# Second attention's score transposes from TensorE to VectorE, paired scores, and a first batch in half chunks

## Chip, core and metric

The kernel runs on one core of one Trainium2 chip. The metric is the device time in microseconds of one execution.

## What is computed

Four batches of 8 heads, 576 queries, 64 dimensions, 32 pack vectors. First attention lets the packs attend to keys and values, second attention lets the queries attend to the packed result; the outcome is 2304 rows of 512. Two feed-forward layers of width 2048 follow, one with softplus, one with h times sigmoid(h). All inputs are fp32, and the weights come as 64-bit words that the kernel turns into fp32.

```
p_packed = sm_attn(p, k, v)
out = sm_attn(q, p_packed, p_packed)
x = out.transpose(0, 2, 1, 3).reshape(B * S, H * D)
g = softplus(x @ w_in);  x = g @ w_out
g = h * sigmoid(h) with h = x @ w_in2;  out = g @ w_out2
```

## The kernel before

Everything is kept transposed, with features on partitions and tokens along the free dimension. Layer 0 works on 8 blocks of 288 tokens (two a batch), layer 1 on blocks of 480. Each layer makes four passes f over the ff width, each with four chunks j of 128 (`GJ`). A unit is (layer, pass, block); a *step* is one chunk of one unit, and `run_steps` (L514) walks them. Step s emits six or twelve h matmuls (`emit_in`, L338) of its own chunk, then the y matmuls of one output quarter dm of the *previous* unit (`emit_out`, L378: four chunks with three matmuls each, 12). ScalarE applies the activation and makes the high part gh (`act_scalar`, L361), VectorE the low part gl (`act_vector`, L373), and `finish_out` (L393) copies or adds y into ya. So y of a unit needs gh and gl of all its chunks, and y starts in step 4. The tiles h and y have two PSUM buffers each.

In layer 0 the second attention's output is never formed: the matrix ax holds the normalised attention weights (32 packs x 4 head pairs on the 128 partitions, two head parities r), in a high and a low part, and `packed` (L317) multiplies each batch's pack vectors pt into the weights w_in, which gives vw. h is then vw times ax: (lo, hi), (hi, lo), (hi, hi), two matmuls each.

`att1(b)` (L168) computes scores of a parity with 8 matmuls of 64 x 32 x 288, takes the row maximum on VectorE, the exponential on ScalarE, transposes on TensorE (`turn`, L198), copies back (`turned`, L204; tile et has one buffer), weighs the values (`weigh`, L210) and turns the normalised result into pt. `att2(blk)` (L265) computes scores with the queries on 96 partitions (24 matmuls of 64 x 96 x 32), subtracts the maximum over the packs, exponentiates, sums, normalises (L284 to L295), and turns the result back with six TensorE transposes (L303); ScalarE copies the high part to ax (L308) and VectorE subtracts for the low part (L310). The scores' and transposes' PSUM tiles all come from one pool of two double banks (`two_banks`).

The work beside the steps is written as generators that yield the name of a point; `plan` (L91) puts them on an agenda by step, and within a step the points run as A0, h, PE, y, activation, A1, D0, D1, A2, D, then gl, then y's copy or addition. Weights are loaded by DMA some five steps before `conv_w` (L109) converts them: three integer passes on VectorE, and for all but the first layer's w_in a high and a low half. `plan_all` (L436) holds the table of steps. Ahead of step 0 stand att1(0), att2(0), att2(1), the first `packed` and eight weight conversions; the first four steps are put in order by an automatic scheduler (`NAUTO`), the rest stand as written. Att1(b) for b of 2 and 3 is planned for steps 8b-10 to 8b-5, att2 of its two blocks for 8b-4 to 8b.

Of the kernel before, what the change touches and what calls it, by code (L numbers as in the profile page):

```python
# [28 lines left out]
QT = 96  # L29
NQ = 3  # L30

N0 = NQ * QT
# [13 lines left out]
def body(ctx, tc, kT, vv, qT, pT, wi1, wo1, wi2, wo2, out):  # L46
# [25 lines left out]
    units = [(L, f, blk) for L in range(2) for f in range(NPASS) for blk in range(len(BLOCKS[L]))]  # L72
    US = {u: i for i, u in enumerate(units)}
    NS = GJ * len(units)
    at = lambda L, f, blk, i=0: GJ * US[L, f, blk] + i
    PER = [GJ * len(b) for b in BLOCKS]
    base = lambda L, f: at(L, f, 0)
# [82 lines left out]
    def load_q(blk):  # L160
        qt = att.tile([P, NQ, NK, QT], F32, name="qt", bufs=2)
        nc.sync.dma_start(out=qt, in_=qT[blk])
        qts[blk] = qt
# [4 lines left out]
    def att1(b):  # L168
# [5 lines left out]
        def scores(r):  # L174
            pz, kt = kts[b]
            s1[r] = two_banks()
            rows = slice(64 * r, 64 * r + 64)
            for half in range(2):
                for k in range(NK):
                    nc.tensor.matmul(  # L180
                        s1[r][32 * k:32 * k + 32, half, :HS], lhsT=pz[rows, k, :],
                        rhs=kt[rows, k, half * HS:(half + 1) * HS], start=True, stop=True,
                    )
# [20 lines left out]
        def turned(r):  # L204
            et[r] = att.tile([P, KC, P], F32, name="et")
# [16 lines left out]
        scores(0)  # L222
        yield "D"
        top(0)
        yield "A0"
        exp(0)
        yield "PE"
        scores(1)
        yield "D"
        top(1)  # L230
        yield "A0"
        exp(1)
        yield "PE"
        turn(0)
        yield "A1"
        turned(0)
        yield "D"
        nc.vector.tensor_copy(et[0][:64, 4, :], s1[0][:64, 1, :P])
        yield "PE"
        turn(1)  # L240
# [3 lines left out]
        yield "A1"  # L244
        turned(1)
        yield "D"
        nc.vector.tensor_copy(et[1][:64, 4, :], s1[1][:64, 1, :P])
        yield "PE"
# [16 lines left out]
    def att2(blk):  # L265

        b = blk // 2
        G = NQ * NK
        yield "PE"
        qt, pt = qts[blk], pts[b]  # L270
        tq = two_banks()
        for i in range(NQ):
            for k in range(NK):
                for r in range(NR):
                    rows = slice(64 * r, 64 * r + 64)
                    c = (i * NK + k) * NP
                    nc.tensor.matmul(  # L277
                        tq[:QT, r, c:c + NP], lhsT=qt[rows, i, k, :], rhs=pt[rows, k * NP:(k + 1) * NP],
                        start=True, stop=True,
                    )  # L280
        yield "D"
        tqv = tq[:QT, :, :G * NP].rearrange("q r (g p) -> q r g p", p=NP)
        mx = att.tile([QT, 2, NR, G], F32, name="mx", bufs=2)
        nc.vector.tensor_reduce(out=mx[:, 0], in_=tqv, axis=AX.X, op=ALU.max)  # L284
        ee = att.tile([QT, NR, G, NP], F32, name="ee", bufs=2)
        nc.vector.tensor_tensor(  # L286
            out=ee, in0=tqv, in1=mx[:, 0].unsqueeze(3).to_broadcast([QT, NR, G, NP]), op=ALU.subtract
        )
        yield "A0"
        nc.scalar.activation(out=ee, in_=ee, func=AF.Exp, scale=SCALE)  # L290
        yield "D"
        nc.vector.tensor_reduce(out=mx[:, 1], in_=ee, axis=AX.X, op=ALU.add)
        nc.vector.tensor_scalar(out=mx[:, 1], in0=mx[:, 1], scalar1=1e-9, scalar2=None, op0=ALU.add)
        nc.vector.reciprocal(out=mx[:, 1], in_=mx[:, 1])
        nc.vector.tensor_tensor(  # L295
            out=ee, in0=ee, in1=mx[:, 1].unsqueeze(3).to_broadcast([QT, NR, G, NP]), op=ALU.mult
        )
        yield "PE"
        tb = two_banks()
        ef = ee.rearrange("q r g p -> q r (g p)")  # L300
        for i in range(NQ):
            for r in range(NR):
                nc.tensor.transpose(  # L303
                    tb[:, r, i * QT:(i + 1) * QT], ef[:, r, i * P:(i + 1) * P], ident[:QT, :QT]
                )
        yield "A1"
        cols = slice(blk * N0, (blk + 1) * N0)
        nc.scalar.activation(out=ax[:, :NR, cols], in_=tb[:, :, :N0], func=AF.Copy)  # L308
        yield "D"
        nc.vector.tensor_tensor(  # L310
            out=ax[:, NR:, cols], in0=tb[:, :, :N0], in1=ax[:, :NR, cols].bitcast(F32), op=ALU.subtract
# [26 lines left out]
    def emit_in(s):  # L338
        L, f, blk = units[s // GJ]
        j = GJ * f + s % GJ  # L340
# [20 lines left out]
    def act_scalar(s, h):  # L361
        L, f, blk = units[s // GJ]
# [11 lines left out]
    def act_vector(s, gt, gh, gl):  # L374
        nc.vector.tensor_tensor(out=gl, in0=gt, in1=gh.bitcast(F32), op=ALU.subtract)  # L375
        gs[s] = gh, gl

    def emit_out(s):  # L378
        u, dm = s // GJ - 1, s % GJ
        L, f, blk = units[u]  # L380
        n = BLOCKS[L][blk][1]
        y = ps.tile([P, 512], F32, name="y")[:, :n]
        c = slice(dm * P, (dm + 1) * P)
        for jj in range(GJ):
            gh, gl = gs[GJ * u + jj]
            wh, wl = whl["o", L * NF + GJ * f + jj]
            for i, (w, g) in enumerate(((wl, gh), (wh, gl), (wh, gh))):
                nc.tensor.matmul(  # L388
                    y, lhsT=w[:, c], rhs=g, start=(jj == 0 and i == 0), stop=(jj == GJ - 1 and i == 2)
                )  # L390
        return y

    def finish_out(s, y):  # L393
        u, dm = s // GJ - 1, s % GJ
        L, f, blk = units[u]
        c, n = BLOCKS[L][blk]
        acc = ya[:, dm, c:c + n]
        if f == 0:
            if L or s % 2:
# [5 lines left out]
        if f == NPASS - 1:  # L405
# [14 lines left out]
    vstep, when = {}, {}  # L420
    for f in range(NPASS):
        for b in range(B):
            for i in range(2):
                if f or b:
                    vstep[b, 2 * f + i] = at(0, f, 2 * b) + i - (3 if f else 4)
# [8 lines left out]
    PRE_W = [("i", n) for n in range(4)] + [("o", n) for n in range(4)]  # L434

    def plan_all():  # L436

        for n, s in zip((*(("i", n) for n in range(4, 8)), *(("o", n) for n in range(4, 8))),
                        (21, 23, 26, 27, 25, 29, 31, 33)):
            when[n] = s  # L440
        for f in range(1, NPASS):
            for d, s in enumerate((6, 10, 26, 27)):
# [16 lines left out]
        for b in range(1, B):  # L459
            t = 8 * b  # L460
            if b > 1:
                plan_load(lambda b=b: load_k(b), t - 16)
                plan_load(lambda b=b: load_v(b), t - 13)
                plan(att1(b), range(t - 10, t - 4))
            for i in range(2):
                plan_load(lambda i=i, b=b: load_q(2 * b + i), t - 10 + i if b > 1 else i)
# [5 lines left out]
    POINTS = "A0", "PE", "A1", "D0", "D1", "A2", "D"  # L472
# [15 lines left out]
    load_w("i", 2)  # L488
    load_w("i", 3)
    load_q(1)  # L490
    first = Item(att1(0))
    for p in ("PE", "D", "A0", "PE", "D"):
        first.run(p)
    load_k(1)
    for n in range(4):
        load_w("o", n)
# [3 lines left out]
    load_v(1)  # L500
    at_once(conv_w("i", 0), conv_w("i", 1))
    at_once(packed(0, 0), att2(0))
    at_once(conv_w("i", 2), conv_w("i", 3))
    at_once(packed(0, 1), att2(1))
    second = Item(att1(1))
    for p in ("PE", "D", "A0", "PE", "D"):
        second.run(p)
    for s in range(4):
        agenda.setdefault(s, []).append(second)
    at_once(*(conv_w("o", n) for n in range(2)))  # L510
    at_once(*(conv_w("o", n) for n in range(2, 4)))
    plan_all()

    def run_steps(steps):  # L514
        for s in steps:
# [7 lines left out]
            go = lambda p: [i.run(p) for i in items]  # L523
            go("A0")
# [3 lines left out]
            if s >= GJ:  # L528
# [65 lines left out]
```

## Time and profile before

| | before |
|---|---|
| median of 3 runs | 830.63 us (829.61 to 831.14) |
| profiled execution, its own time | 829.38 us |
| its span | 827.6 us |
| TensorE busy | 794.7 us, 96% |
| VectorE busy | 454.8 us, 55% |
| ScalarE busy | 360.7 us, 44% |
| mean granted TensorE clock | 0.977 |

The span runs from the first to the last instruction of the profiled execution. Busy shares are averages over stages with different limits. A TensorE matmul on fp32 data that are not fp32r shows as two instructions, so a group of 8 is listed as x16. The granted clock of 1.0 is 2.4 GHz, 0.5 is 1.2 GHz.

### The profile page before, as it was taken

To read this page: it belongs to the slowest core of one execution; us is meant where nothing else is said; L and a number is where in the kernel's file an instruction comes from. 1 tells how busy PE (TensorE), PEld (TensorE's weight loads), DVE (VectorE), ACT (ScalarE), POOL (GpSimd) and SP (SyncE) were. 2 spreads that over 40 slices of the span, in tenths; PEclk is the share of its full clock that TensorE was granted. 3 is DMA by queue.
4 is the path that set the end of the run, shared out by engine and by line. 5 is a ranking of instruction groups with operands and counts; after the bars stand their busy time and mean duration, and the time that the engine had idled before them with its cause. 6 is when DMAs were issued, how large, how long until landed. Compare 5 with 4: busy or idle time off the path is not lost.

```text
span 827.6 us, 13403 instructions
## 1 busy us (share of the span) xinstructions
PE 794.7 (96%) x5660; PEld 714.4 (86%) x5660; DVE 454.8 (55%) x856; ACT 360.7 (44%) x687; POOL 0.7 (0%) x6
## 2 busy tenths in 40 slices
PE   5679999999999999999999999999999999999998
PEld 3557878899999999999998889988899888988887
DVE  4746456866664665477754432555556554543332
ACT  3457576754544454466644443433323332322220
POOL 0000000000000000000000000000000000000000
PEclk9569999999999999999999999999999999999999
DMA  9533224020112011201102003200032000001111
GB/s 349 210 116 119 88 106 179 2 103 1 38 67 102 2 39 64 104 1 42 62 20 82 1 1 102 88 15 1 4 99 101 1 1 26 26 12 49 48 48 74
DMA packets 15932, 53.62 MB, mean 65 GB/s; under 512 B 1792, under 2 KB 4864, under 8 KB 15360
## 3 DMA queue, kind: packets, MB, share of 16 engines
q1 hardware_dynamic: 15872, 52.77, 17.6%
q8 instruction: 44, 0.72, 0.4%
q14 instruction: 16, 0.13, 0.0%
HBM read 48.05 MB, written 4.72 MB: 64 GB/s over the span
## 4 chain that ended last, share of the span: by engine, by line
PE 91%; DVE 4%; ACT 3%; issue 1%; DMA 1%; SPq 0%; DVEq 0%; ACTq 0%
PE y L388 48%; PE h L358 35%; PE psa L277 2%; PE psa L324 2%; PE psa L180 1%; PE psa L216 1%; DMA kt<-kT 1%; ACT L368 1%; PE psa L303 1%; PE psa L202 0%; ACT L193 0%; DVE mx L284 0%; DVE ee L286 0%; DVE wx L121 0%; ACT e L193 0%
## 5 line engine op out<-in xcount | busy, mean ns | idle before, releaser
L388 PE MATMUL y<-gh,w 128*128 128x288 f32 (+2 forms) x1664 | 427.9, 328 | 0.0
L388 PEld LDWEIGHTS y<-gh,w 128*128 128x128 f32 x1664 | 291.4, 188 | 29.5 <-issue 10.9
L388 PE MATMUL y<-gl,w 128*128 128x288 f32 (+2 forms) x832 | 269.9, 324 | 0.2 <-DVE gl L375 0.2
L368 ACT ACTIVATE gt<-h 128x288 f32<-128x288 f32 (+2 forms) x208 | 96.9, 466 | 289.4 <-PE h L358 289.0
L388 PEld LDWEIGHTS y<-gl,w 128*128 128x128 f32 x832 | 157.0, 189 | 8.4 <-DVE gl L375 0.5
L358 PE MATMUL h<-ax,w 128*128 128x480 f32 (+1 forms) x640 | 160.1, 372 | 0.0
L375 DVE TENSOR_TENSOR gl<-gt,gh 128x288 fp32r<-128x288 f32 (+2 forms) x208 | 108.7, 523 | 72.4 <-ACT gh L371 71.0
L370 DVE TENSOR_TENSOR gt<-h,gt 128x480 f32<-128x480 f32 (+1 forms) x80 | 51.0, 638 | 175.8 <-ACT gt L368 175.8
L358 PEld LDWEIGHTS h<-ax,w 128*128 128x128 f32 x640 | 118.9, 188 | 15.6
L371 ACT ACTIVATE gh<-gt 128x288 fp32r<-128x288 f32 (+2 forms) x208 | 104.1, 501 | 60.3 <-DVE gt L370 56.3
L358 PE MATMUL h<-ax,vw 128*128 128x288 f32 x768 | 126.3, 301 | 4.0 <-ACT gt L368 4.0
L358 PEld LDWEIGHTS h<-ax,vw 128*128 128x128 f32 x768 | 111.7, 193 | 6.1 <-ACT gt L368 4.3
L404 DVE TENSOR_TENSOR ya<-y,ya 128x288 f32<-128x288 f32 (+2 forms) x156 | 81.7, 524 | 17.6 <-PE y L388 17.4
L358 PE MATMUL h<-xl,w 128*128 128x480 f32 (+1 forms) x320 | 79.9, 371 | 0.0
L358 PEld LDWEIGHTS h<-xl,w 128*128 128x128 f32 x320 | 59.4, 188 | 8.0
L138 ACT ACTIVATE w<-wx 128x512 fp32r<-128x512 f32 x48 | 30.3, 632 | 42.8 <-DVE wx L127 42.8
L117 ACT ACTIVATE wc<-wraw 128x512 f32<-128x512 f32 x64 | 42.3, 661 | 8.7 <-DMA wraw<-wi 6.4
L121 DVE SCALAR_TENSOR_TENSOR wx<-wraw,wx 128x512 int32<-128x512 int32 x64 | 44.3, 692 | 2.0
L127 DVE SCALAR_TENSOR_TENSOR wx<-wc,wx 128x512 int32<-128x512 int32 x48 | 33.2, 691 | 3.0
L332 DVE TENSOR_TENSOR vw<-psa,vw 128x512 fp32r<-128x512 f32 x32 | 21.9, 686 | 21.5 <-ACT vw L330 21.5
L140 DVE TENSOR_TENSOR w<-wx,w 128x512 fp32r<-128x512 f32 x48 | 32.8, 683 | 1.0 <-ACT w L138 1.0
L120 DVE TENSOR_SCALAR wx<-wraw 128x512 int32<-128x512 int32 x64 | 26.8, 418 | 7.8 <-DMA wraw<-wi 7.8
(49 smaller groups left out, 316.8 us busy)
## 6 DMA issues: line engine op xcount, KB each, us to landing
wraw<-wi SPq DMA_DIRECT2D x32, 512.0 KB, 4.3
wraw<-wo SPq DMA_DIRECT2D x32, 512.0 KB, 5.5
kt<-kT SPq DMA_DIRECT2D x8, 576.0 KB, 4.9
qt<-qT SPq DMA_DIRECT2D x8, 576.0 KB, 3.7
vt<-vv SPq DMA_DIRECT2D x4, 1040.0 KB, 7.1
yT<-ya SPq DMA_DIRECT2D x16, 240.0 KB, 2.0
yT<-ya SPq DMA_DIRECT2D x4, 192.0 KB, 1.9
vt<-vv SPq DMA_DIRECT2D x4, 130.0 KB, 7.1
```

The lines of the kernel that those rows point to most:

```text
L117: nc.scalar.mul(c, hw.bitcast(F32), 2.0 ** -112)
L121: nc.vector.scalar_tensor_tensor(out=x, in0=hw, scalar=-(2 ** 31), in1=x, op0=ALU.bitwise_and, op1=ALU.bitwise_or)
L127: nc.vector.scalar_tensor_tensor(out=y if first else x, in0=c.bitcast(I32), scalar=3, in1=x, op0=ALU.logical_shift_left, op1=ALU.bitwise_or,)
L138: nc.scalar.activation(out=hi, in_=x, func=AF.Copy)
L140: nc.vector.tensor_tensor(out=lo, in0=x, in1=hi.bitcast(F32), op=ALU.subtract)
L358: nc.tensor.matmul(h, lhsT=w, rhs=x, start=(i == 0), stop=(i == len(mm) - 1))
L368: nc.scalar.activation(out=gt, in_=h, func=AF.Sigmoid if L else AF.Softplus)
L370: nc.vector.tensor_tensor(out=gt, in0=h, in1=gt, op=ALU.mult)
L371: nc.scalar.activation(out=gh, in_=gt, func=AF.Copy)
L375: nc.vector.tensor_tensor(out=gl, in0=gt, in1=gh.bitcast(F32), op=ALU.subtract)
L388: nc.tensor.matmul(y, lhsT=w[:, c], rhs=g, start=(jj == 0 and i == 0), stop=(jj == GJ - 1 and i == 2))
L404: nc.vector.tensor_tensor(out=acc, in0=y, in1=acc, op=ALU.add)
```

## The change

Five things change.

1. Att2 computes its scores the other way round: packs on partitions (32 for each of four head pairs), 288 queries along the free dimension, 8 matmuls of 64 x 32 x 288 in place of 24 of 64 x 96 x 32. VectorE turns 32x32 squares (tile tr, 128 x 576), so that the packs lie along the free dimension for maximum, sum and product, and turns them back (tile tb, in SBUF). The six transposes on TensorE are gone, and ax is made from tb. The exponential moves from point A0 to A1; sum, product and second transpose stand at D0, which is now the first point of a step.
2. Att1's scores of both parities are computed in one group whose matmuls alternate between the row halves, and its maxima, exponentials, turns, copies and weighing go in pairs; et has two buffers.
3. Batch 0's first pass is done in half groups: units of two chunks, so steps 0 to 7 are blocks 0 and 1 with chunks 0 and 1, then with chunks 2 and 3. A step of such a unit emits two output quarters of y, with two chunks each. y starts in step 2, and in steps 8 to 11 a y group has 6 matmuls. The second half is added to ya on VectorE.
4. Ahead of step 0 only chunks 0 and 1 of both weights are converted; chunks 2 and 3 follow at steps 0 to 4, and att1(1) starts earlier. The loads are issued in that order.
5. `act_vector` runs before point D. Some conversions in `plan_all` move by a step.

```diff
+    group = lambda f: tuple(range(GJ * f, GJ * f + GJ))
+    units = [(0, js, blk) for js in (group(0)[:2], group(0)[2:]) for blk in range(2)]
+    units += [
+        (L, group(f), blk) for L in range(2) for f in range(NPASS)
+        for blk in range(2 * (not L and not f), len(BLOCKS[L]))
+    ]
...
     def att2(blk):
...
+        for k in range(NK):
+            for r in range(NR):
+                rows = slice(64 * r, 64 * r + 64)
+                nc.tensor.matmul(
+                    tq[32 * k:32 * k + 32, r, :N0], lhsT=pts[b][rows, k * NP:(k + 1) * NP], rhs=qts[blk][rows, k, :],
+                    start=True, stop=True,
+                )
+        yield "D"
+
+        tr = att.tile([P, NR * G, NP], F32, name="tr", bufs=2)
+        mx = att.tile([P, 2, NR * G], F32, name="mx", bufs=2)
+        wide = [P, NR * G, NP]
+        nc.vector.transpose(tr.rearrange("q (r g) p -> q r (g p)", r=NR), tq[:, :, :N0])
+        nc.vector.tensor_reduce(out=mx[:, 0], in_=tr, axis=AX.X, op=ALU.max)
+        nc.vector.tensor_tensor(out=tr, in0=tr, in1=mx[:, 0].unsqueeze(2).to_broadcast(wide), op=ALU.subtract)
+        yield "A1"
+        nc.scalar.activation(out=tr, in_=tr, func=AF.Exp, scale=SCALE)
+        yield "D0"
+        nc.vector.tensor_reduce(out=mx[:, 1], in_=tr, axis=AX.X, op=ALU.add)
...
+        nc.vector.tensor_tensor(out=tr, in0=tr, in1=mx[:, 1].unsqueeze(2).to_broadcast(wide), op=ALU.mult)
+        tb = att.tile([P, NR, N0], F32, name="tb", bufs=1)
+        nc.vector.transpose(tb, tr.rearrange("q (r g) p -> q r (g p)", r=NR))
+        yield "A1"
+        cols = slice(blk * N0, (blk + 1) * N0)
+        nc.scalar.activation(out=ax[:, :NR, cols], in_=tb, func=AF.Copy)
...
-        for n, s in zip((*(("i", n) for n in range(4, 8)), *(("o", n) for n in range(4, 8))),
-                        (21, 23, 26, 27, 25, 29, 31, 33)):
+        for n, s in (("i", 4), 21), (("i", 5), 23), (("i", 6), 25), (("i", 7), 26):
+            when[n] = s
+        for n, s in (("o", 4), 27), (("o", 5), 28), (("o", 6), 30), (("o", 7), 32):
             when[n] = s
...
-    POINTS = "A0", "PE", "A1", "D0", "D1", "A2", "D"
+    POINTS = "D0", "A0", "PE", "A1", "D1", "A2", "D"
```

How the order moves. First TensorE from batch 0's first `packed` (writes psa from w) up to the first y matmuls. Psa<-kt are att1's scores, psa<-pt,qt or psa<-qt,pt att2's, psa<-ident transposes, psa<-vt the weighing. Before:

```order
L324 MATMUL psa<-w,pt 32x256 x8
L277 MATMUL psa<-pt,qt 96x32 x24
L303 MATMUL psa<-ident,ee 128x96 x6
L324 MATMUL psa<-w,pt 32x256 x8
L358 MATMUL h<-ax,vw 128x288
L277 MATMUL psa<-pt,qt 96x32 x24
L358 MATMUL h<-ax,vw 128x288 x22
L303 MATMUL psa<-ident,ee 128x96 x6
L180 MATMUL psa<-kt,pz 32x288 x16
L358 MATMUL h<-ax,vw 128x288 x7
```

And now:

```order
L313 MATMUL psa<-w,pt 32x256 x8
L274 MATMUL psa<-qt,pt 32x288 x8
L187 MATMUL psa<-kt,pz 32x288 x16
L348 MATMUL h<-ax,vw 128x288 x10
L274 MATMUL psa<-qt,pt 32x288 x8
L348 MATMUL h<-ax,vw 128x288 x2
L209 MATMUL psa<-ident,e_310 128x128 x4
...
L383 MATMUL y<-gh,w 128x288 x2
L383 MATMUL y<-gl,w 128x288
L383 MATMUL y<-gh,w 128x288
```

Att1(1)'s scores stand ahead of the first h, its turns right behind two steps of h, and y of step 2 follows; the second `packed` comes later.

Next VectorE in steps 5 to 7 of the new kernel, from the second transpose of scores to the first additions into ya:

```order
L283 STREAM_TRANSPOSE tr<-psa 128x576
...
L289 TENSOR_REDUCE mx<-tr 128x18
L290 TENSOR_SCALAR mx<-mx 128x18
L291 RECIPROCAL mx<-mx 128x18
L292 TENSOR_TENSOR tr<-tr,mx 128x576
L294 STREAM_TRANSPOSE tb<-tr 128x576
L365 TENSOR_TENSOR gl<-gt,gh 128x288
L299 TENSOR_TENSOR ax<-tb,ax 128x2x288
L193 TENSOR_REDUCE sm<-psa 128x1
L194 TENSOR_SCALAR sm<-sm 128x1
L193 TENSOR_REDUCE sm<-psa 128x1
L194 TENSOR_SCALAR sm<-sm 128x1
L400 TENSOR_TENSOR ya<-y,ya 128x288 x2
```

And of the kernel before, the same place, where the product (L295) ends the chain and one parity's maximum is taken a step:

```order
L292 TENSOR_REDUCE mx<-ee 96x24
L293 TENSOR_SCALAR mx<-mx 96x24
L294 RECIPROCAL mx<-mx 96x24
L295 TENSOR_TENSOR ee<-ee,mx 96x768
L284 TENSOR_REDUCE mx<-psa 96x24
L286 TENSOR_TENSOR ee<-psa,mx 96x768
L332 TENSOR_TENSOR vw<-psa,vw 128x512
L375 TENSOR_TENSOR gl<-gt,gh 128x288
L310 TENSOR_TENSOR ax<-psa,ax 128x2x288
L186 TENSOR_REDUCE sm<-psa 128x1
L187 TENSOR_SCALAR sm<-sm 128x1
L375 TENSOR_TENSOR gl<-gt,gh 128x288
```

Step 6 now holds the whole second half of a block's softmax with a transpose, both of att1's maxima and two additions behind them.

## Rows read from the trace of the kernel before

**Rows 1.** The page: busy time and share of TensorE; its granted clock in 40 slices.
```profile
PE 794.7 (96%) x5660; PEld 714.4 (86%) x5660; DVE 454.8 (55%) x856; ACT 360.7 (44%) x687; POOL 0.7 (0%) x6
...
PEclk9569999999999999999999999999999999999999
```
**Rows 2.** Busy time by stretch: us, PE, PEld, DVE, ACT, POOL busy (count), clock, DMA share, GB/s.
```profile
20.00:29.00 9.00, 3.13 (x40) 3.00 (x38) 6.26 (x11) 1.75 (x3) 0.00 (x0) 0.50 1.03 390
30.00:39.00 9.00, 9.00 (x82) 7.62 (x81) 6.76 (x12) 5.60 (x10) 0.00 (x0) 0.51 0.23 80
...
38.00:40.00 2.00, 1.69 (x10) 1.46 (x9) 2.00 (x5) 1.98 (x3) 0.00 (x0) 0.79 0.32 129
...
66.52:169.45 102.93, 96.80 (x1122) 86.56 (x1122) 66.27 (x129) 69.10 (x119) 0.00 (x0) 1.00 0.26 93
...
169.45:827.60 658.15, 654.59 (x4049) 595.33 (x4047) 352.37 (x658) 260.89 (x521) 0.00 (x0) 1.00 0.13 45
```
**Rows 3.** The chain that ended last, in order of time: start, us, what.
```profile
63.55 2.97 PE y L388 x12
...
101.24 2.16 PE psa L277 x48
103.40 0.59 PE psa L324 x16
103.99 1.79 PE y L388 x12
...
106.57 0.50 PE psa L303 x6
107.07 1.10 PE psa L180 x16
...
169.45 0.79 PE h L358 x6
170.25 1.59 PE y L388 x12
```
**Rows 4.** Waits of TensorE from 66.52 to 169.45: total us, times, longest.
```profile
PE psa L202 <- ACT e L193: 2.5, 2, 1.3
PE psa L303 <- DVE ee L295: 1.8, 1, 1.8
PE psa L303 <- DVE ee L286: 1.1, 1, 1.1
PE psa L202 <- DVE ax L310: 0.8, 2, 0.4
```
**Rows 5.** Timeline of the head: start, us, instructions [idle before, releaser].
```profile
15.03 0.60 ACT L206 ACTIVATE et<-psa 128x512 f32<-128x512 f32 x1 [1.90 <-PE psa L216]
...
18.15 1.00 PE L324 MATMUL psa<-w,pt 64*32 64x256 f32 x16 [0.37 <-ACT pt L263]
...
19.08 4.05 PE L277 MATMUL psa<-pt,qt 64*96 64x32 f32 x48
...
31.29 0.61 PE L358 MATMUL h<-ax,vw 128*128 128x288 f32 x1
```
**Rows 6.** Groups of VectorE from 66.52 to 169.45: busy, mean ns, idle before.
```profile
L375 DVE TENSOR_TENSOR gl<-gt,gh 128x288 fp32r<-128x288 f32 x27 | 12.1, 448 | 2.7 <-ACT gh L371 2.7
...
L121 DVE SCALAR_TENSOR_TENSOR wx<-wraw,wx 128x512 int32<-128x512 int32 x7 | 4.9, 694 | 0.2
...
L310 DVE TENSOR_TENSOR ax<-psa,ax 128x576 fp32r<-128x576 f32 x6 | 4.5, 758 | 14.4 <-ACT ax L308 14.4
...
L120 DVE TENSOR_SCALAR wx<-wraw 128x512 int32<-128x512 int32 x7 | 2.9, 420 | 0.0
...
L254 DVE TENSOR_TENSOR px<-psa,sm 128x128 f32<-128x128 f32 x2 | 0.6, 292 | 0.1
```
**Rows 7.** Groups of ScalarE from 72 to 171.8 us: busy, mean ns.
```profile
L371 ACT ACTIVATE gh<-gt 128x288 fp32r<-128x288 f32 x27 | 12.0, 445 | 0.9
...
L368 ACT ACT_TABLE_LOAD x7 | 9.0, 1283 | 0.1
```

More of the change, by code (lines that the diff above doesn't have):

```diff
@@ L234, in att1 @@
         turn(0)
+        turn(1)
         yield "A1"
         turned(0)
+        turned(1)
         yield "D"
-        nc.vector.tensor_copy(et[0][:64, 4, :], s1[0][:64, 1, :P])
+        for r in range(NR):
+            nc.vector.tensor_copy(et[r][:64, 4, :], s1[r][:64, 1, :P])
         yield "PE"
-        turn(1)
         po = two_banks()
         weigh(0)
[L244 to L248, printed above, removed]
         weigh(1)
@@ L267, in att2 @@
         b = blk // 2
-        G = NQ * NK
+        G = N0 // NP
         yield "PE"
-        qt, pt = qts[blk], pts[b]
         tq = two_banks()
[L272 to L280, printed above, removed]
@@ L281, in att2 @@
-        yield "D"
[L282 to L290, printed above, removed]
@@ L291, in att2 @@
-        yield "D"
-        nc.vector.tensor_reduce(out=mx[:, 1], in_=ee, axis=AX.X, op=ALU.add)
+        for k in range(NK):
+            for r in range(NR):
+                rows = slice(64 * r, 64 * r + 64)
+                nc.tensor.matmul(
+                    tq[32 * k:32 * k + 32, r, :N0], lhsT=pts[b][rows, k * NP:(k + 1) * NP], rhs=qts[blk][rows, k, :],
+                    start=True, stop=True,
+                )
+        yield "D"
+        tr = att.tile([P, NR * G, NP], F32, name="tr", bufs=2)
@@ L338, in emit_in @@
     def emit_in(s):
-        L, f, blk = units[s // GJ]
-        j = GJ * f + s % GJ
+        u, i = steps[s]
+        L, js, blk = units[u]
+        j = js[i]
         c, n = BLOCKS[L][blk]
@@ L417, in split_x @@
         )
[L420 to L425, printed above, removed]
+    when = {}
+    vstep = {(b, 2 * f + i): base(0, f) + 8 * b - 4 + i for f in range(NPASS) for b in range(B) for i in range(2)}
+    vstep[0, 1] = 3
+    del vstep[0, 0]
     def last_use(k, n):
@@ L487, in body @@
     load_q(0)
-    load_w("i", 2)
-    load_w("i", 3)
+    load_w("o", 0)
+    load_w("o", 1)
     load_q(1)
     first = Item(att1(0))
-    for p in ("PE", "D", "A0", "PE", "D"):
+    for p in "PE", "D", "A1":
         first.run(p)
     load_k(1)
-    for n in range(4):
-        load_w("o", n)
+    for n in 2, 3:
+        load_w("i", n)
     while first.due:
@@ L500, in body, with run_steps @@
     load_v(1)
+    for n in 2, 3:
+        load_w("o", n)
     at_once(conv_w("i", 0), conv_w("i", 1))
     at_once(packed(0, 0), att2(0))
-    at_once(conv_w("i", 2), conv_w("i", 3))
-    at_once(packed(0, 1), att2(1))
     second = Item(att1(1))
-    for p in ("PE", "D", "A0", "PE", "D"):
+    for p in "PE", "D":
         second.run(p)
-    for s in range(4):
+    at_once(conv_w("o", 0), conv_w("o", 1))
+    second.run("A1")
+    at_once(att2(1))
+    for s in 1, 2, 3:
         agenda.setdefault(s, []).append(second)
-    at_once(*(conv_w("o", n) for n in range(2)))
-    at_once(*(conv_w("o", n) for n in range(2, 4)))
+    for k, n, s in ("i", 2, 0), ("i", 3, 1), ("o", 2, 3), ("o", 3, 4):
+        plan(conv_w(k, n), (s, s + 1))
     plan_all()
-    def run_steps(steps):
-        for s in steps:
+    def run_steps(first, end):
+        for s in range(first, end):
             if s == base(0, 1):
```

125 lines of the change are left out of this document (54 added, 71 removed).

## Prediction

> **What bounds the kernel now.** I read the page's busy table first, then the TensorE clock by slices, then busy time by stretch, and last the chain of waits. TensorE is busy for 96% of the span, and its clock is below full speed only in the first slices [rows 1]. The stretches cut the span in three [rows 2, 3]. The *head* runs to 66.52 us, where step 5's h begins (a step is one pass of `run_steps`: one h group, one y group, and whatever attention is planned there). The *middle* runs from there to 169.45 us, step 32's h: 102.93 us in which attention and dense work share TensorE at full clock. The *rest* is 658.15 us of dense matmuls with TensorE busy for 654.59. A dense step costs 0.79 us for six h matmuls and 1.59 us for twelve y matmuls, so 0.132 us a matmul [rows 3]. Nothing in the change touches the rest's matmuls, and I carry its 658.15 us over as they are: VectorE has 352 us of work there and ScalarE 261 [rows 2], so planning weight conversions a step earlier or later, or running the `D0` point first, hides behind TensorE. If that cover failed it would show as y matmuls waiting for `gl` after step 32.
>
> The middle holds 6.2 us in which TensorE waits, every time in front of a transpose (`turn`, or att2's back-transpose) [rows 4]. The head is a chain of latencies: the clock shows 0.50 from 20 to 29 us [rows 2], and TensorE waits for VectorE, ScalarE's table loads and DMA in turn.
>
> **The middle, part by part.** Att2's scores took 48 instructions and 2.16 us a block [rows 3]. Now they are 16 instructions of 288 columns, alternating between the two row halves and the four column strips. The row nearest to that is `packed`, 16 instructions of 256 columns in the same pattern, 0.59 us [rows 3]; by columns this gives 0.66. The bound from above is `scores` of one parity, 16 of 288 columns that do not alternate rows, 1.10 us [rows 3]; the one from below is `packed`'s 0.59. I take 0.66: 1.5 us less for each of 5 blocks, **-7.5**. The back-transposes on TensorE go: 0.50 us [rows 3], up to 0.7 elsewhere, 6 of them, **-3.6**. Att1's scores cost 2 x 1.10 a batch and become one group of 32 alternating instructions, 1.33 by the same price: -0.87 for each of two batches, **-1.7**. Starting batch 0 in half groups leaves the matmul count alone but brings y forward: at the end of step 4, 24 more y matmuls are done than before, and steps 8 to 11 hold six instead of twelve: 24 x 0.132, **-3.2**. The 6.2 us of waits go, because the transposes they stood before are gone or come two steps after their exponentials: **-6.2**. Sum -22.2.
>
> What is late next is VectorE, which takes over the turning. Per att2 block it gains two transposes of 128x576 from 32x32 squares, an operation that the trace lacks. Nearest is the pass over 128x576, 0.76 us [rows 6], and I take that. Below, the floor is the 0.29 of a 128x128 pass [rows 6]; above I allow 2.7 us, the point of the last rival. The other passes shrink from 96x768 to 128x576, so a block's total on VectorE hardly moves.
>
> 128x128 takes 0.292 us and 128x576 0.758 [rows 6]: a pass has a fixed part, and 4.5 times the width costs 2.6 times the time. A transpose that paid the whole 0.292 for each 128 columns would take 1.31; that is a rival below. The Trainium skill (VectorE: DVE Perf Modes, The three transpose paths) gives 311 ns for a 128x128 transpose in 32x32 squares; taken by squares, ours would be an estimated 1.40 us and the sum some 8 us later, and no row here shows the operation.
>
> With that price VectorE falls behind in two places. **Steps 4 to 7** (times from step 4's h): its first `gl` can start 1.7 us in, after h 0.8 and ScalarE's two passes of about 0.45 [rows 7]. Then, small operations left out, step 4 has gl 0.45, transpose, max and subtract 2.28, vw 0.69, ya 0.45 [rows 6]: 3.9. Step 5 has the same and a weight half at 0.69: 4.5. Step 6 has sum, product and second transpose 2.28, gl 0.45, ax 0.76, two maxes 1.5, and only then the first of two ya additions at 0.45: 5.4. That ends at 15.5. TensorE needs 3.84 (h 0.8, scores 0.66, packed 0.59, y 1.79) for steps 4 and 5 each, 3.9 for step 6, and 0.8 for step 7's h, so it stands at 12.4 before a y whose PSUM buffer this addition frees (y has two buffers, step 6 fills both). Wait: 3 to 4 with the small operations, **+4**. **Steps 20 to 26**: attention of the last batch meets weight conversions (0.42 + 0.69 + 0.69 = 1.8 a chunk [rows 6]) planned at 21, 23, 25 and 26, ahead of `gl` in VectorE's queue. Steps 20 to 25 add up there to 3.9, 5.3, 4.3, 2.2, 4.3 and 2.2 (first halves of a softmax with vw, second halves with ax, a conversion in every other), 22.2, plus 1.7 of lead-in; TensorE needs step 25's gl after two steps of 3.84, four of 2.38, an h and two thirds of a y, 19.1: **+5**. The period between, without conversions, lacks about 1 us, and the rest I put at 0.5. New waits **+10.5**; bounds 3 (buffers absorb most) and 15. The middle becomes 102.9 - 22.2 + 10.5 = **91.2 us**.
>
> **The head.** To `pt` of batch 0, with which `packed` starts at 18.15 [rows 5], the gain is small: the second copy of `turned` no longer waits 1.9 us for `weigh(0)` (`et` has two buffers [rows 5]), but the second exponential now waits for both maxes and a conversion pass. I count -0.7: 17.5. Packed takes about 1.0 [rows 5] and att2(0)'s scores 1.2 at this clock instead of 4.05 [rows 5]. Then VectorE is the chain without a gap: vw from 18.9, and up to the end of the second transpose come vw at 0.69, six passes over 128x576 at 0.76 (two of them transposes), five conversion passes, 0.42 and 4 x 0.69, and two small ones: 8.9 us, so 27.8; ScalarE's copy makes it 28.5, where h starts (31.29 before [rows 5]). From there to step 4 the order hands over between ScalarE, with four table loads of 1.28 us [rows 7] between exponentials and softplus, and VectorE: the second exponential of att1(1) at 34, gl of step 0 at 36.5 and of step 1 at 39.6, weigh at 40 to 42, att2(1)'s ax at 43.9, px at 45.5, pt and vw(0,1) at 48 to 52. Step 4 itself is 3.8 us at full clock, 6.9 at half. All at full clock it ends at 53.0, all at half at 58.7. In the kernel before, the clock was low through a stretch without a gap from 30 on and came back at its end, at a mean of 0.79 between 38 and 40 us [rows 2]; the new one is mostly busy from 28.5 to 36 and from 40 to 49, so I expect full clock for most of the second half: **54.5 us** against 66.52.
>
> **Sum.** 54.5 + 91.2 + 658.15 = 803.9 us of span. The profiled execution took 829.38 with a span of 827.6, so 1.8 lies outside: **805.6 us**, 23.8 below its own time. It stands 1.25 below the median of the runs, 830.63, within their spread.
>
> **Rivals.**
> *VectorE keeps up.* The buffers take the lag and the waits stay at 3 to 4 us. For it: the kernel before has VectorE at 66.27 us of work in 102.93 [rows 2]. Against: the two places above are local. 805.6 - 7 = 798.6.
> *The clock stays at half* past step 4: TensorE has less to do in the head's gaps, and y shows 2.97 us for twelve matmuls at half clock against 1.79 at full [rows 3]. Step 4 ends at 58.7 and one or two later steps run slow under VectorE's lag: 811 to 812. The Trainium skill (TensorE: Matmul & The Clock Gate, What's actually happening) has the slow clock as the default that activity releases; the trace agrees, 0.50 over 20 to 29 us with TensorE busy 3.13 of 9.
> *Transposes at 1.31 us.* 0.55 more for each: four on the head's chain, some eight in the two places: +6.6, 812. For it that the squares are turned one by one; against, that a fixed part need not come back for each.
> *The pairs do not run side by side*, so the change does not do what it says: scores at 1.10 and 2 x 1.10. 5 x 0.44 + 2 x 0.87 in the middle and some 2.5 in the head: 812.
> *Slower.* One mechanism: the transpose of 4-byte elements is a slow operation. Of 16 transposes about 12 are on the path; 23.8/12 is 2.0 above 0.76, so from 2.7 us each the gain is gone, and at 3.2 the kernel takes about 835. For it only that no row shows the operation.
>
> **Chances.** The forecast 0.50, VectorE keeps up 0.20, half clock 0.12, transposes at 1.31 us 0.10, no pairs 0.04, slower 0.04. A measurement of this kernel can tell about 0.2% (1.7 us) from no change. All cases but the last are faster by more than that; between them lies almost nothing: faster 0.95, same 0.01, slower 0.04. The range reaches from the case in which VectorE keeps up, with the head at 53, 796, to the dear transposes and part of a slow clock, 816.
>
> **What would show it.** Right: transposes near 0.76 us; att2's scores near 0.66 and att1's near 1.33 at full clock; step 5's h near 54.5 us and step 32's near 146; y matmuls waiting for ya additions at step 7, and for gl at steps 22 to 26; no wait from step 32 on. Wrong: a transpose of 1.3 us or more; clock 0.5 beyond 60 us; or waits in the rest, which would mean that the moved conversions are not hidden.

## The result, and the profile after

| | before | after |
|---|---|---|
| median, beside each other | 830.88 us (829.61 to 831.36, 4 runs) | **806.2 us** (805.34 to 806.7, 4 runs) |
| ratio, 95% interval | | 0.9704 [0.9687, 0.9721] |
| profiled execution, its own time | 829.38 us | 806.7 us |
| its span | 827.6 us | 804.6 us |

The forecast was 805.6 us, with a range of 796 to 816. By stretches of the profiled execution, each measured from the h of a step as in the forecast:

| stretch | before | forecast | after |
|---|---|---|---|
| head, to step 5's h | 66.52 | 54.5 | 56.50 |
| middle, to step 32's h | 102.93 | 91.2 | 90.42 |
| rest | 658.15 | 658.15 | 657.68 |
| outside the span | 1.8 | 1.8 | 2.1 |

The page after, busy time and TensorE's granted clock in 40 slices, beside [rows 1]:

```profile
PE 773.2 (96%) x5356; PEld 689.8 (86%) x5356; DVE 465.6 (58%) x880; ACT 353.1 (44%) x683; POOL 0.7 (0%) x6
...
PEclk9989999999999999999999999999999999999999
```

TensorE has the same share of the span as before, at 23 us less: such a page shows that TensorE still bounds the kernel, and nothing of where the time went. The stretches do, beside [rows 2]. (TensorE's clock is shown too high up to some 34 us, here and below; the last section tells from what this is seen.) Busy time by stretch (start:end and length in us, then PE, PEld, DVE, ACT, POOL busy with their counts, clock, DMA share, GB/s):

```profile
0.00:56.50 56.50, 35.73 (x410) 22.52 (x411) 36.96 (x76) 28.85 (x47) 0.70 (x6) 0.94 0.70 257
51.04:56.50 5.46, 5.46 (x52) 3.85 (x53) 3.12 (x5) 1.97 (x4) 0.00 (x0) 0.69 0.30 108
52.00:54.00 2.00, 2.00 (x34) 0.67 (x33) 0.69 (x2) 0.85 (x2) 0.00 (x0) 0.50 0.00 0
56.50:146.92 90.42, 83.09 (x902) 72.26 (x902) 73.35 (x148) 62.71 (x115) 0.00 (x0) 0.98 0.29 106
68.00:72.00 4.00, 3.64 (x16) 3.65 (x17) 2.14 (x6) 2.89 (x4) 0.00 (x0) 0.59 0.00 0
146.92:804.60 657.68, 654.34 (x4049) 595.03 (x4047) 355.32 (x658) 261.55 (x522) 0.00 (x0) 1.00 0.13 45
```

In the middle TensorE's busy time fell by 13.71 us (96.80 to 83.09), while its idle time rose, from 6.13 to 7.33. What it waited for there is new from the first line to the last; in [rows 4] every wait stood before a transpose. Waits of TensorE from 56.50 to 146.92 (us in total, times, longest):

```profile
PE y L383 <- DVE ya L400: 2.9, 1, 2.9
PE h L348 <- ACT ax L297: 1.7, 1, 1.7
PE y L383 <- DVE ya L398: 1.2, 2, 1.0
PE psa L223 <- DVE et L244: 0.6, 2, 0.3
PE y L383 <- DVE gl L365: 0.5, 1, 0.5
PE h L348 <- DVE ax L299: 0.3, 1, 0.3
```

The operation that no row of before showed, among VectorE's groups of the middle (busy us, mean ns of one, idle before):

```profile
L294 DVE STREAM_TRANSPOSE tb<-tr 128x576 f32<-128x576 f32 x6 | 4.7, 778 | 0.2
L292 DVE TENSOR_TENSOR tr<-tr,mx 128x576 f32<-128x576 f32 x6 | 4.5, 757 | 0.2
L289 DVE TENSOR_REDUCE mx<-tr 128x18 f32<-128x576 f32 x6 | 4.5, 746 | 0.1
L283 DVE STREAM_TRANSPOSE tr<-psa 128x576 f32<-128x576 f32 x5 | 3.9, 776 | 0.0
```

A transpose of squares takes nearly what any pass over 128x576 takes (776 and 778 ns against 746 and 757), from PSUM and from SBUF alike. Step 7's wait, read back along the chain of waits (start, us, what):

```profile
64.75 0.69 ACT ax L297
...
65.47 0.76 DVE ax L299
66.23 0.68 DVE sm L193
...
67.08 0.68 DVE sm L193
...
67.94 0.38 DVE ya L400
...
68.36 2.97 PE y L383 x12
```

Ax, both maxima of att1, and only then the addition that frees the buffer of y: VectorE's queue of step 6, in the order that the forecast had laid out. Behind the wait the twelve y matmuls take 2.97 us, the price at half clock [rows 3], and the window from 68 to 72 shows 0.59.

In the head the same happens once more. Timeline of TensorE there (start, us, instructions, [idle before, releaser]):

```profile
47.74 0.66 PE L313 MATMUL psa<-w,pt 64*32 64x256 f32 x16
51.04 1.32 PE L348 MATMUL h<-ax,vw 128*128 128x288 f32 x6 [2.64 <-DVE vw L321]
52.28 1.21 PE L274 MATMUL psa<-qt,pt 64*32 64x288 f32 x16
```

Step 4's h stands behind batch 0's second `packed` and VectorE's part of vw, and that part behind ScalarE's, which from 46.94 to 49.61 us loads a table and does the softplus of two other steps. TensorE idles 2.64 us before this h, and the whole of step 4 then takes 5.46 us, with a clock of 0.50 from 52 to 54 us, where 3.84 were counted at full clock.

### The profile page after: what moved, and what is told of

It reads as the page before. It is cut to its first block, busy times and chain, and to the rows that moved or that the text cites. A ratio compares the mean times of both kernels' runs of the same rounds, so it can differ in the third digit from the quotient of the medians.

```text
span 804.6 us, 12782 instructions
## 1 busy us (share of the span) xinstructions
PE 773.2 (96%) x5356; PEld 689.8 (86%) x5356; DVE 465.6 (58%) x880; ACT 353.1 (44%) x683; POOL 0.7 (0%) x6
## 4 chain that ended last, share of the span: by engine, by line
PE 88%; DVE 7%; ACT 2%; DMA 1%; issue 0%; SPq 0%; DVEq 0%; ACTq 0%
PE y L383 48%; PE h L348 36%; PE psa L313 2%; PE psa L223 1%; DMA wraw<-wi 1%; DMA kt<-kT 1%; ACT ax L297 1%; DVE tb L294 1%; DVE tr L292 1%; DVE ax L299 1%; DVE mx L284 1%; DVE vw L321 1%; DVE tr L283 1%; DVE mx L289 1%; DVE sm L193 1%; DVE tr L285 0%
## 5 line engine op out<-in xcount | busy, mean ns | idle before, releaser
L400 DVE TENSOR_TENSOR ya<-y,ya 128x288 f32<-128x288 f32 (+2 forms) x164 | 85.2, 520 | 22.8 <-PE y L383 22.7
L123 ACT ACTIVATE wc<-wraw 128x512 f32<-128x512 f32 x64 | 42.3, 662 | 10.5 <-DMA wraw<-wi 7.0
L396 ACT ACTIVATE ya<-y 128x288 f32<-128x288 f32 (+2 forms) x36 | 17.4, 484 | 14.1 <-PE y L383 13.9
```

Of the source, the lines that this page charges most:

```text
L123: nc.scalar.mul(c, hw.bitcast(F32), 2.0 ** -112)
L400: nc.vector.tensor_tensor(out=acc, in0=y, in1=acc, op=ALU.add)
```

## Experiments

Two theories of why the forecast fell so close stood at the start. **A**, the forecast's: the time comes from att2's scores and back-transposes, VectorE's transposes cost a plain pass, and what is left over are two local lags of VectorE, at steps 4 to 7 and 20 to 26, and the late vw of step 4. **B**, the rival: several terms are wrong and cancel; the gain is made by something else, the pairs or the half groups, and the lags only shift when one mends them. All differences below are to the changed kernel's 806.2 us.

| kernel | us, median (range, runs) | ratio to before | to 806.2 |
|---|---|---|---|
| e1 additions to ya first | 809.21 (808.93 to 810.16, 5) | 0.9736 [0.9723, 0.9749] | +3.0 |
| e2 conversions early | 805.69 (805.52 to 806.51, 4) | 0.9694 [0.9681, 0.9707] | -0.5 |
| e3 packed early | 801.31 (801.22 to 802.04, 4) | 0.9641 [0.9628, 0.9654] | -4.9 |
| e4 every transpose twice | 811.56 (811.45 to 811.8, 4) | 0.9763 [0.975, 0.9776] | +5.4 |
| e5 row halves in fours | 798.64 (798.27 to 799.02, 4) | 0.9605 [0.9592, 0.9619] | -7.6 |
| e6 three moves | 797.99 (797.25 to 798.48, 5) | 0.9598 [0.9585, 0.9611] | -8.2 |
| e7 att2 as before | 843.49 (840.22 to 844.8, 4) | 1.0139 [1.0117, 1.016] | +37.3 |
| e8 no half groups | 801.51 (800.66 to 801.81, 4) | 0.9638 [0.9625, 0.9651] | -4.7 |
| e9 att2's halves in fours | 806.37 (805.84 to 806.7, 4) | 0.9697 [0.9683, 0.9711] | +0.2 |
| e10 e5 with two moves | 796.38 (795.6 to 798.08, 4) | 0.958 [0.9563, 0.9597] | -9.8 |
| e11 e5 with three moves | **796.11** (795.62 to 797.02, 4) | 0.9575 [0.9561, 0.959] | -10.1 |
| e12 e8 in fours, conversions early | 803.12 (802.11 to 803.4, 4) | 0.9654 [0.9638, 0.9671] | -3.1 |

Only e9 fell within its theory's range and e2 within its rival's. E3, e6, e10 and e11 missed their theory's by about a microsecond or less; e1, e4, e5, e7, e8 and e12 came out further off, and e1, e5, e7, e8 and e12 outside both of their ranges on the same side. Parts 4 and 5 of the change were not taken out by themselves.

Where stretches of two runs are compared, a profiled execution is a single one, and its head varies. E1, e2 and e9 have the changed kernel's instructions in the same order on TensorE up to step 5, and there step 5's h begins at 55.4, 54.7 and 55.6 us against 56.5; e10 has e5's order and stands 2.9 us behind it. So a difference in the head is certain only to 2 or 3 us.

**e4, the price of a transpose.** Each of the two transposes is issued twice.

```diff
-        nc.vector.transpose(tr.rearrange("q (r g) p -> q r (g p)", r=NR), tq[:, :, :N0])
+        for _ in range(2):
+            nc.vector.transpose(tr.rearrange("q (r g) p -> q r (g p)", r=NR), tq[:, :, :N0])
...
```

> Every transpose of 32x32 squares is done twice (the second writes the same values): 16 more passes of 0.78 us, 12.5 us of VectorE. Theory (about 12 of the 16 stand on the path, in the head and in the two places where VectorE lags): 8 to 11 us slower, 814 to 817. Rival (VectorE has slack at 58% busy): 4 us of the head at most, 808 to 810.

The two groups of transposes in the middle stand at the same price, and the middle alone grew, from 90.42 us to 100.13:

```profile
L296 DVE STREAM_TRANSPOSE tb<-tr 128x576 f32<-128x576 f32 x12 | 9.3, 778 | 0.4
L284 DVE STREAM_TRANSPOSE tr<-psa 128x576 f32<-128x576 f32 x11 | 8.6, 779 | 0.2
...
52.08:152.21 100.13, 84.62 (x902) 73.44 (x901) 83.66 (x162) 62.78 (x115) 0.00 (x0) 0.97 0.27 99
```

9.7 us for 12 more transposes (23 against 11) is 0.81 each, no less than the 0.78 that one takes: VectorE's time in the middle does lie on the path, as theory A has it. The total of +5.4 is smaller because the head came out 4.3 us shorter (step 5's h at 52.08 in the timeline, against 56.34). The first four steps are put in order by the automatic scheduler, and the longer transposes changed its order. That was the first sign of what e5 showed.

**e1 and e2, the two lags of VectorE.** In e1 `finish_out` stands ahead of point D in all steps from 4 on, so that the additions no longer queue behind the maxima:

```diff
-            go("D")
             for y in ys:
                 finish_out(s, *y)
+            go("D")
```

> From step 4 on, y's copy or addition is issued ahead of the work at point D. Theory (VectorE's queue holds y's buffer at step 7, and the clock falls in the gap): step 7's wait of 2.9 us for the ya addition is gone, the clock shows no 0.5 between 68 and 72 us, and the time is 3 to 5 us below the changed kernel's 806.2, 801 to 803. Rival (VectorE is short of time as a whole, and the order of its queue only moves the wait): the same 3 us turn up in front of h or at att1's turns, 805.5 to 807.

Waits of TensorE from 40 to 150 us in e1, the three that matter:

```profile
PE psa L313 <- DVE vw L321: 4.3, 3, 1.5
...
PE psa L187 <- DVE vw L321: 1.3, 1, 1.3
...
PE y L383 <- DVE ya L400: 0.7, 1, 0.7
```

The wait of step 7 is gone; the 0.7 stands before step 8's y. But what now stands behind the additions, vw and the steps of the softmax, came late in other steps, and the middle grew by 3.9 us (90.42 to 94.29). On an engine that is late as a whole, the wait was not mended by moving its cause ahead everywhere; the time changed the line that it is shown at. In e2 the conversions of chunks 4 and 5 of w_in go from steps 21 and 23 to 17 and 18:

```diff
-        for n, s in (("i", 4), 21), (("i", 5), 23), (("i", 6), 25), (("i", 7), 26):
+        for n, s in (("i", 4), 17), (("i", 5), 18), (("i", 6), 25), (("i", 7), 26):
```

> The conversions of w_in chunks 4 and 5 move from steps 21 and 23 to 17 and 18, where VectorE has little to do. Theory (they stand ahead of gl and of att2's passes in VectorE's queue in steps 21 to 26): TensorE's 3.5 us of waits between 109 and 131 us shrink to about 1, the time falls by 2 to 3 us to 803 to 804. Rival (the last batch's att2 chain is late by itself, through ScalarE's table loads and its own passes): the waits stay, 805.5 to 807.

Steps 20 to 25 went from 20.41 us to 17.84 (h of step 20 to h of step 26), so the lag that the forecast saw there is real. It was given back at step 18, in front of the weighing, where the clock fell behind the wait. In all the time is that of the changed kernel, within the spread of the runs. Timeline, and a stretch of e2:

```profile
103.47 2.43 PE L223 MATMUL psa<-vt,et 128*32 128x65 f32 x80 [2.18 <-DVE et L244]
...
104.00:108.00 4.00, 4.00 (x70) 3.42 (x59) 2.36 (x6) 0.34 (x1) 0.00 (x0) 0.57 0.02 4
```

**e3, step 4's wait.** The second `packed` of batch 0 a step earlier:

```diff
-    vstep[0, 1] = 3
+    vstep[0, 1] = 2
```

> Batch 0's second packed product is planned for step 2 instead of 3, so that vw(0,1) no longer comes behind the softplus of steps 2 and 3 on ScalarE. Theory (the head's end hangs on that chain): step 4's h no longer waits 2.6 us for vw, the clock does not fall before step 4, and the time falls by 2.5 to 4 us, to 802 to 803.5. Rival (step 4 needs gl of steps 2 and 3 and pt of batch 1, which are as late): the wait moves to att2's scores or to y, within 1 us of 806.2.

No wait for vw is left in the head, step 4 starts at 46.80 instead of 51.04, and its clock stays up:

```profile
45.22 0.27 PE L259 MATMUL psa<-ident,px 128*128 128x128 f32 x1
46.80 0.95 PE L348 MATMUL h<-ax,vw 128*128 128x288 f32 x6
...
46.80:50.50 3.70, 3.70 (x53) 2.95 (x52) 3.02 (x7) 3.04 (x8) 0.00 (x0) 1.00 0.35 107
```

4.9 us: about the wait and the slow clock together (2.64 and 1.8), and more than the head's miss.

**e5 and e9, the pairs.** In both score groups the row half becomes the outer loop inside each group, so that four matmuls of one half are followed by four of the other; in e9 this is done in att2 alone.

```diff
-        for k in range(NK):
-            for r in range(NR):
+        for r in range(NR):
+            for k in range(NK):
```

> The changed kernel with both groups of scores in the other loop order: first all matmuls of one row half, then all of the other. Nothing else moves. Theory (the matmuls of the two row halves run side by side only when they alternate): att2's 16 instructions take about 1.1 us instead of 0.66 and att1's 32 about 2.2 instead of 1.33 at full clock; 3 to 5 us slower, 809 to 811, a little less where VectorE is late anyway. Rival (the column strips alone give the rate): 805.5 to 807.

It came out 7.6 us *faster*, against both theories. The groups themselves take the same time as with strict alternation. Chain of e5, and its stretches to step 5's h and to step 32's:

```profile
74.01 0.65 PE psa L274 x16
...
81.61 1.58 PE psa L187 x32
...
0.00:48.34 48.34, 30.39 (x408) 19.54 (x409) 34.52 (x74) 26.81 (x45) 0.70 (x6) 0.89 0.82 294
48.34:138.42 90.08, 81.76 (x902) 70.55 (x901) 74.75 (x150) 62.70 (x115) 0.00 (x0) 1.00 0.30 110
```

In the changed kernel the same group of 32 runs from 89.85 to the next y at 91.44, 1.59 us. The middle is 90.08 against 90.42; nearly all of the gain lies in the head (step 5's h at 48.34 against 56.34 in the timelines), where the instructions stand in another order: the y matmuls of the first steps come ahead of the last h matmuls before step 5, which are then one run of 18 matmuls, and batch 1's weighing and px come earlier (px's transpose at 41.06 instead of 47.54), so that no h waits for vw there. Timeline of e5:

```profile
41.06 0.30 PE L259 MATMUL psa<-ident,px 128*128 128x128 f32 x1 [0.86 <-DVE px L254]
...
42.36 3.27 PE L348 MATMUL h<-ax,vw 128*128 128x288 f32 x18 [0.41 <-ACT ax L297]
```

Which of the two was the cause, the loop or the order, e9 tells: it has every engine's instructions in the changed kernel's order, with att2's loops as in e5.

> Att2's scores row half after row half, att1's still alternating; every engine's instructions stand in the order of the changed kernel. Theory, that the 7.6 us gained without alternation come from the order in which the first four steps then fall: 806 (805 to 807.5), step 5's h near 56.5, the 16-instruction group of scores still 0.65 at full clock. Rival, that alternating score groups cost time themselves: 5 blocks in the middle and 2 in the head run faster, 801 to 803.

806.37: att2's loop is worth nothing. As att1's group takes the same time either way (1.58 and 1.59), what is left for the 7.6 is the order. It changed only where att1's loops were swapped as well (e5); att1's alone were not run. Why the scheduler then chose otherwise is not visible in a trace and stays open.

**e8 and e12, the half groups.** In e8 batch 0 is done in whole groups of four chunks again, with all eight conversions ahead of step 0, the loads in that order and the later points of att1(1) from step 0 on; the rest is as changed.

```diff
-    units = [(0, js, blk) for js in (group(0)[:2], group(0)[2:]) for blk in range(2)]
-    units += [
-        (L, group(f), blk) for L in range(2) for f in range(NPASS)
-        for blk in range(2 * (not L and not f), len(BLOCKS[L]))
-    ]
+    units = [(L, group(f), blk) for L in range(2) for f in range(NPASS) for blk in range(len(BLOCKS[L]))]
...
```

> The changed kernel without half groups: units of four chunks throughout, all eight conversions of the first chunks ahead of step 0 and loads in the order of the kernel before; att2 and att1 as changed. Theory (half groups let TensorE start y two steps earlier beside VectorE's conversions, and that is worth the 24 matmuls, 3.2 us, and some of the head, less the 4.8 us that step 7 loses): 2 to 8 us slower, 808 to 814. Rival (y forward is paid back at steps 7 to 11): 805 to 807.

Faster by 4.7, where the half groups had been counted as a gain. Stretches and waits of e8's middle:

```profile
0.00:51.61 51.61, 31.07 (x386) 19.42 (x387) 36.19 (x75) 23.35 (x41) 0.70 (x6) 0.80 0.76 281
51.61:141.02 89.41, 85.97 (x926) 75.35 (x926) 70.61 (x141) 63.24 (x117) 0.00 (x0) 0.98 0.30 108
...
PE h L344 <- ACT ax L293: 1.7, 1, 1.7
PE psa L219 <- DVE et L240: 0.7, 2, 0.3
PE y L379 <- DVE ya L394: 0.6, 3, 0.2
```

The middle holds 24 matmuls more (926 records against 902) and is still 1.0 us shorter, because TensorE idles 3.4 us there instead of 7.3: without two output quarters a step there is no step 7 that waits for its additions. Half groups thus moved 24 matmuls out of the middle and bought a wait with them, and in the changed kernel a slow clock behind it. (E8's middle has a slow clock too, at another place: 0.57 from 118 to 122 us.) How much of the head's 4.9 us is theirs is not settled, because the head's order changed as well, and e12 shows what that can do: e8 with the loops of e5 and the conversions at 15 and 19.

> No half groups, neither score group alternates, the conversions of chunks 4 and 5 at 15 and 19. Theory: without half groups y does not stand in the first four steps, so the order that gained 8.2 in the head has no counterpart and only the conversions' 0.5 to 1 comes: 800 to 801.5. Rival: the gains add, 792 to 794.

803.12, 1.6 slower than e8. The loops that came with a gain of 7.6 us with half groups came with a longer head here: step 5's h starts at 55.1 instead of 51.61, behind a wait of 4.0 us for softplus that ends at 41 us and a clock of 0.50 from 41 to 55, while the middle, 88.46, is 0.95 shorter than e8's.

**e7, att2 on TensorE again.** Att2 of the kernel before (with its layout of q), everything else as changed.

> The changed kernel with the second attention of the kernel before (24 matmuls of scores, turned back by TensorE), in the new order of steps and halves. Theory (att2 is the larger part of the gain: 2.16 against 0.66 us of scores in 5 blocks, 6 back-transposes and the waits before them in the middle, twice that in the head where the clock is low): 15 to 22 us slower, 821 to 828. Rival (half chunks, pairs and the new order of the head give most of the gain): below 815.

+37.3, slower than the kernel before and far outside both expectations. Waits of TensorE over the whole span:

```profile
PE psa L305 <- DVE ee L297: 15.1, 4, 6.4
PE psa L305 <- DVE ee L288: 8.0, 3, 3.3
```

The back-transposes wait 23.1 us for VectorE; in the kernel before the same transposes wait 8.9 us over its whole span. It seems that the new order of points has no place where a TensorE transpose has something to cover it. So the run doesn't price att2 by itself. It does show that the new order is a loss without part 1; whether part 1 gains without the new order was not run.

**e6, e10 and e11, what adds up.** E6 takes e3's move, puts the additions first in steps 6 and 7 alone, and the two conversions at 15 and 19.

```diff
-    vstep[0, 1] = 3
+    vstep[0, 1] = 2
...
-        for n, s in (("i", 4), 21), (("i", 5), 23), (("i", 6), 25), (("i", 7), 26):
+        for n, s in (("i", 4), 15), (("i", 5), 19), (("i", 6), 25), (("i", 7), 26):
...
+            early = s in (6, 7)
...
```

> Three moves on the changed kernel: batch 0's second packed product at step 2; y's additions ahead of point D in steps 6 and 7 alone, where two of them stand behind both maxima of att1; conversions of w_in chunks 4 and 5 at steps 15 and 19, away from the copies that the weighing of step 18 waits for. Theory (each wait of TensorE in steps 4 to 26 comes from one named piece of work ahead in a queue): 801.3 with the first alone, less 2.9 of wait and about 1.9 of slow clock at step 7, less 2.6 at steps 20 to 26: 794 to 797. Rival (VectorE has no more room, the waits only move): 799 to 802.

Waits of TensorE from 40 to 150 us in e6:

```profile
PE psa L223 <- DVE et L244: 1.5, 2, 1.1
PE y L383 <- DVE ya L398: 1.4, 2, 1.2
PE y L383 <- DVE ya L400: 0.8, 1, 0.8
```

Aimed at the one place, the additions' move works: step 7's wait of 2.9 is gone, 0.8 stands before step 8's y, and most of e1's new waits do not come. E10 is e5 with the moves of e6 but for `packed`; e11 adds that one.

> Neither score group alternates; in steps 6 and 7 the additions to ya stand ahead of point D; the conversions of chunks 4 and 5 stand at 15 and 19. Theory: the wait of 3.0 before step 7's y falls to under 1 and the waits of steps 20 to 26 fall by 1 to 2, 4 in all from 798.6: 794 to 795.5. Rival, that the additions only push VectorE's other work back, as when they stood first in all steps: 797.5 to 800.

> As the kernel with both score groups unalternated and the three tables moved, and packed(0,1) at step 2 too. Theory: the order of the first steps without alternation already takes away the wait for vw that this move removed (step 4's h starts early there), so it adds little: within 1 us of the kernel without this move, 793.5 to 796. Rival: the gains add, 789 to 791.5.

E10's profiled execution was its slowest, 798.08, with a head of 51.25; so the middles are to be compared. Stretches from step 5's h to step 32's in the timelines, of e10 and of e11:

```profile
51.25:138.15 86.90, 81.78 (x903) 70.52 (x902) 73.89 (x150) 62.60 (x115) 0.00 (x0) 1.00 0.31 114
```

```profile
48.03:135.51 87.48, 81.97 (x902) 70.58 (x901) 74.43 (x150) 62.73 (x115) 0.00 (x0) 1.00 0.31 113
```

The two moves in the middle are worth 2.6 to 3.2 us (90.08 before them), less than the 4 expected. `packed` a step earlier, worth 4.9 alone, adds 0.3 within overlapping ranges to the order of e5, and leaves the head at 48.03 against 48.34: what this move mends, the late vw, the order of e5 had mended already. E11 at 796.11 has the lowest median of the case, with e10 within its range, 10.1 below the changed one and 35.2 below the one before beside it (831.27).

## Why the prediction was right

**Att2's scores, -7.5: right**, by the price of the group; no run takes part 1 out alone. 0.65 us at full clock (the chain of e5) against 0.66, for 2.16 before. The price was taken from `packed`, and the bound from above, 1.10 for a group that keeps to one row half [rows 3], was rightly not taken. For the price both row halves have to occur in one group, but need not alternate one by one: in fours they cost the same (e5, e9). The Trainium skill (TensorE: Matmul & The Clock Gate, Part 3: Packing small matmuls) says that matmuls on different row and column tiles of the array run at the same time while they start and end in program order. The traces agree as far as they go: 16 instructions over two halves in 0.65, 16 over one in 1.10.

**Back-transposes, -3.6: right**, by the counts: none is left on TensorE but att1's.

**Att1's scores, -1.7: too large.** The group of 32 takes 1.59, not 1.33, so 0.6 a batch came instead of 0.87. Why 32 cost more than twice the 0.65 of 16 is not shown.

**24 y matmuls brought forward, -3.2: right as a count of TensorE's work, wrong as a gain.** The middle holds them no more, as e8's 926 against 902 records show. But they come with the wait of step 7 and a slow clock behind it, and e8 without half groups is 4.7 us faster.

The four terms make -16.0; TensorE's busy time fell by 13.7. The difference is 0.5 in att1's scores and about 1.9 in step 7 and 8 at half clock (y at 2.97 for 1.59, h at 1.3 for 0.8), which the forecast did not have. It need not come with the wait: in e5 step 7's y waits 2.96 us, the clock stays at 1.00, and the y takes 1.89.

**Waits gone, -6.2, and new waits, +10.5.** The old ones went. Of the new ones 7.3 came. Step 7's wait was named with its place and its cause, at +4; it was 2.9, and 4.8 with the clock. The +5 of steps 20 to 26 were 3.5, as h waiting for ax (2.0), y for an addition (1.0) and only 0.5 as y for gl: the conversions delay whatever stands behind them in the queue. The lag is the conversions' all the same (e2: 2.6 us less in those steps without them).

**Transposes at 0.76: right**, at 0.776 and 0.778, and in the middle all of it on the path (e4). The Trainium skill (VectorE: DVE Perf Modes, The three transpose paths) has 311 ns for a 128x128 bf16 transpose; by squares that was an estimated 1.40 here, and the traces differ: 0.78 for fp32 data, about a plain pass over the same width. So both rivals that made the transpose dear fell.

**The head, 54.5: 2.0 short.** One step failed: it put the clock at full "for most of the second half" and step 4 at 3.8 us. By its own times TensorE was busy to 49 and vw(0,1) came at 48 to 52, so a gap before step 4's h was in them, but no low clock behind it was counted: 2.64 us of wait, then 0.50 of clock, and 5.46 us for step 4, the same in e1, e2 and e9. The other part is the start, where `packed` was counted at 17.5 and h at 28.5: they began at 18.81 and 29.50. That part is not the kernel's but this execution's: with the same order of instructions to there, `packed` begins at 18.04, 17.44 and 18.32 in e1, e2 and e9, and h at 28.28, 27.68 and 28.57, so that the forecast start stands and step 5's h falls between 54.7 and 56.5. Which part of the change took the 10.0 us out of the head no run tells apart; e5 shows that another order of the same instructions alone moves it by some 8 us.

**The rest, unchanged: right.** 657.68 against 658.15, with TensorE busy for 654.34 and no wait in it. The moved conversions and the earlier `D0` hide there.

So six terms of the sum stand, and those that failed (head +2.0, slow clock in the middle +1.9, att1's scores +0.5, new waits -3.2, and -0.5 in the rest) cancel to 0.7 us of span. That the total came so close is therefore in part luck; the mechanisms of att2, the transposes and the lags are not. Theory A holds for att2, the transposes and the lags; theory B holds for the half groups, which the forecast had credited.

## What to carry to other kernels

Where a few steps are put in order by an automatic scheduler, an edit that changes nothing in cost can move the time by more than the edit that one is testing: before a difference is put down to an edit, compare the order of the instructions, and run a version that has the edit in the old order. A unit that splits work finer to start the consumer earlier must also pay for its additional accumulations, here on the engine that was then late (how much of e8's gain this is stays open). And a wait that is mended everywhere at once (e1) can come back at another line; mended at its one place (e6) it stayed away here.

## What the runs showed of the hardware that was not expected

Single waits of TensorE were often followed by a low clock. It idled 2.64 us before step 4's h and was granted 0.50 from 52 to 54 us; it idled 2.9 us before step 7's y, and 68 to 72 show 0.59; in e2 it idled 2.18 us and 104 to 108 show 0.57. Step 4 took 1.8 us longer than in e3, where the wait is missing (5.46 against 3.70). From the start of step 7's y to the second h behind it went 4.81 us, against 3.31 at full clock in e5. In e2 step 18 took 7.93 us instead of 4.68, 1.8 of it by the longer wait and 1.4 by the clock.

The length of the wait did not decide it. In e5 TensorE idled 2.96 us before step 7's y and the clock stayed up; a wait of 1.73 us for ax before step 24's h was followed by 1.00 in the changed kernel (124 to 128) and by 0.57 in e8. Nor did work at once bring the clock back: in e12, behind the wait of 4.0 us, 41 to 55 show 0.50 with TensorE busy for 12.26 of 14 us, and the kernel before has its 0.51 from 30 to 39 with TensorE never idle [rows 2]. What does decide it stays open. Stretches of e5 and of e8:

```profile
61.00:65.00 4.00, 3.85 (x29) 3.85 (x30) 3.12 (x9) 3.51 (x6) 0.00 (x0) 1.00 0.00 0
```

```profile
118.00:122.00 4.00, 3.84 (x17) 3.85 (x18) 3.76 (x10) 3.92 (x6) 0.00 (x0) 0.57 0.02 6
```

A clock in a profile has to be held against the matmuls beside it. The changed kernel's profile shows 1.00 for all of its first 41 us, and every other run has a low stretch there. But its first ten h matmuls take 2.77 us from 29.50, as they do in e9 from 28.57, where the clock is shown at 0.50; at the 0.132 us of a matmul at full clock they would take 1.3. Stretches of the changed kernel and of e9 with the same eleven instructions:

```profile
29.50:32.20 2.70, 2.70 (x11) 2.42 (x11) 2.70 (x8) 2.16 (x3) 0.00 (x0) 1.00 0.44 176
```

```profile
28.57:31.27 2.70, 2.70 (x11) 2.42 (x11) 2.70 (x8) 2.16 (x3) 0.00 (x0) 0.50 0.68 274
```

So TensorE ran at the low level there, the 0.94 over the changed kernel's head is too high, and its head is no proof that few gaps keep the clock up.
